# Moving a cosine product behind the value products, and dealing output products unevenly, in a fused Fourier and gated-layer kernel

## The chip, the core and the metric

The kernel runs on one core of a Trainium2 chip. The core has a matrix engine (TensorE, PE in the profile, with its weight loads as PEld), three engines for elementwise work (VectorE or DVE, ScalarE or ACT, GpSimd or POOL) and SyncE (SP), which issues most transfers. Each engine works through its own queue in order; they wait for each other by semaphores. The metric is the device time in microseconds (us), as the median of several runs.

## The reference

```python
X = np.fft.fft(x, axis=1)              # x: 8 sequences x 3008 rows x 256
X = np.fft.fft(X, axis=2)
x = X.real.reshape(24064, 256)
gate = np.maximum(x @ w_gate, 0.0)     # 256 x 1536
val = x @ w_val                        # 256 x 1536
out = gate * val @ w_out               # 1536 x 256
```

So a two-dimensional Fourier transform, of which the real part is kept, then a gated layer with a ReLU on the gate.

## The kernel before

**Folding.** The transform along the 256 channels is folded into the weights, so that gate and value are made from two arrays for each sequence, U (cosine part of the transform along the rows) and V (sine part): WA and WB are the weights combined with the cosine and sine of the channels, WM is -2 times WB. Row s and its mirror row S-s have the same cosine part and opposite sine parts. So each *tile*, 128 of the 1536 hidden columns by a block of 512 or 481 rows, yields both the rows and their mirror rows: the value of the rows is WA·U + WB·V, and with one more product, the **mirror product** (`mirror`, line 880, WM·V added to the same PSUM bank), it becomes that of the mirror rows. In PSUM a bank holds 128 x 512 numbers; `v` has two banks, `p` two, `o` two, `g` and `d` one each.

**Order of the work.** Sequence b (0 to 7) has three blocks of rows (512, 512, 481; sequence 0 has four smaller segments and another code path), and a block has 12 tiles, numbered from 0. From sequence 1 on, each tile is one call of `slot`, in which parts of four tiles are interleaved by hand: `cur`, whose value is made, `mid`, the next, `nxt`, after it, whose gate is made, and `after`, whose gate is seeded. In TensorE's queue a call puts, in this order:

- the sine product of the gate of `nxt` (`sine_part`, line 1020), which ScalarE copies out (line 1023)
- a first share of **output products** (line 782, 256 columns each): the block before, times w_out. They wait for nothing near by, and are dealt to the tiles by `outs`, of which five eighths, rounded down, go here
- the cosine product of the gate of `nxt` (`cosine_part`, line 1027), onto a seed that ScalarE wrote (`seed`, line 1015)
- where `mid` is *short* (below): its cosine product (`value_cosine`, line 1045)
- the mirror product of the tile before (`pending`, line 880)
- the value products of `cur` (lines 874 and 875)
- the rest of the output products

VectorE follows with the second half of `pending` and the first half of `cur` (both line 910: ReLU of the gate, times the value), then one step of the gate of `nxt` (`both`, line 1031), to which GpSimd adds (line 1032). The mirror product of a tile changes the bank that its first half reads, so it has to wait for that half.

**Short tiles.** In the last four blocks, three tiles each are short: their value takes two products instead of three. ScalarE seeds bank `d` (`seed_value`, line 1041), `value_cosine` adds WA·U and ScalarE keeps twice the result (line 1046); in the tile's own call `value_sine` (line 1050) adds the sine part; the mirror half is made by subtraction (line 1055, VectorE) and a product on GpSimd (line 1056). `outs` is corrected by one or two products around a short tile.

**Other work between tiles.** During the first two blocks of sequences 2 to 6 the row transform of the next sequence is made: after tiles 0, 2, 6, 8 three products each (line 586), and in tiles 3, 4, 9, 10 one *sum* each on VectorE (line 598 and the like). `run_one(evict)` copies a finished output bank to SBUF (line 795), and SP sends it out (line 807).

`per_tile` is the number of output products that wait, divided by 12 and rounded up. A 512-row block leaves 96 of them, 8 a tile; a 481-row block leaves 84 or, when enough remaining rows of several sequences have come together, 96.

Of the kernel before, what the change touches and what calls it, by code (L numbers as in the profile page):

```python
# [34 lines left out]
def kernel(  # L35
# [815 lines left out]
    def run(todo, n):  # L851
        for _ in range(min(n, len(todo))):
            todo.pop(0)()
        if not paired:
            flush()

    def run_one(todo):
        if todo:
            todo.pop(0)()
# [12 lines left out]
    def two(bank, st, i):  # L872

        nc.tensor.matmul(bank[:, 0:st["n"]], lhsT=WA[i][:, st["f"]], rhs=st["us"], start=True, stop=False)  # L874
        nc.tensor.matmul(bank[:, 0:st["n"]], lhsT=WB[i][:, st["f"]], rhs=st["vs"], start=False, stop=True)  # L875

    def mirror(bank, st, i):

        W, v = (WB, st["vm"]) if st["b"] == 0 else (WM, st["vs"])
        nc.tensor.matmul(bank[:, 0:st["n"]], lhsT=W[i][:, st["f"]], rhs=v, start=False, stop=True, skip_group_check=True)  # L880

    def bank(tag):
        return {"g": psG, "p": psP, "v": psV, "d": psD}[tag].tile([128, 512], F32, name=tag, tag=tag)

    def space():
        return rp.tile([128, 512], F32, name="r", tag="r", bufs=12)
# [26 lines left out]
    def second(st):  # L913
        (relu_mult if "s" in st else mult)(st, 1)
        if st["n"] == 481:
            keep_rest(st)
# [5 lines left out]
    def value(st):  # L922
        st["v"] = bank("v")
        two(st["v"], st, 1)

    def gate(st, tag="g"):
        st["g"] = bank(tag)
        two(st["g"], st, 0)
        relu(st)
# [80 lines left out]
    def seed(st, p=None):  # L1010

        if st is None or st["kind"] == "o":
            return
        st["p"] = p or bank("p")
        nc.scalar.activation(st["p"][:, 0:st["n"]], st["c"], ACTF.Copy, scale=b2[:, st["fi"]:st["fi"] + 1])  # L1015

    def sine_part(st):
        n = st["n"]
        st["g"] = bank("g")
        nc.tensor.matmul(st["g"][:, 0:n], lhsT=WM[0][:, st["f"]], rhs=st["vs"], start=True, stop=True)  # L1020
        q = space()
        st["s"] = q, space(), q
        nc.scalar.copy(q[:, 0:n], st["g"][:, 0:n])  # L1023

    def cosine_part(st):
        n = st["n"]
        nc.tensor.matmul(st["p"][:, 0:n], lhsT=WA[0][:, st["f"]], rhs=st["us"], start=False, stop=True, skip_group_check=True)  # L1027
# [15 lines left out]
    def value_cosine(st):  # L1043
        n, st["a"] = st["n"], space()
        nc.tensor.matmul(st["v"][:, 0:n], lhsT=WA[1][:, st["f"]], rhs=st["us"], start=False, stop=True, skip_group_check=True)  # L1045
        nc.scalar.mul(st["a"][:, 0:n], st["v"][:, 0:n], 2.0)
# [5 lines left out]
    def value_second(st):  # L1052
        n = st["n"]
        a = st["a"][:, 0:n]
        nc.vector.tensor_tensor(a, a, st["v"][:, 0:n], op=ALU.subtract)
        nc.gpsimd.tensor_tensor(half_h(st, 1), st["s"][2][:, 0:n], a, op=ALU.mult)
        if n == 481:
            keep_rest(st)

    def slot(cur, mid, nxt, after, outs, fold_us):  # L1060

        outs += cur["short"] + (pending is not None and pending.get("short", False)) - 2 * (mid is not None and mid["short"])
        stop = len(todo_out)

        def out(part):
            run(todo_out, len(todo_out) - stop + outs * part // 8)
        old = nxt is not None and nxt["kind"] == "o"
        new = nxt is not None and nxt["kind"] == "n"
        if old:
            gate(nxt)  # L1070
        lead = cur["lead"]
        out(4 if lead else 0)
        if new and mid["kind"] != "o":
            sine_part(nxt)
        out(4 if lead else 5)
        if new and mid["kind"] == "o":
            sine_part(nxt)
        if new and not lead:
            cosine_part(nxt)
        if not lead:  # L1080
            seed(after)
        if mid is not None and mid["short"]:
            value_cosine(mid)
        if pending is not None and pending.get("short"):
            value_second(pending)
        elif pending is not None:
            mirror(pending["v"], pending, 1)
            second(pending)
        if cur["short"]:
            value_sine(cur)  # L1090
        else:
            value(cur)
        if cur["kind"] == "o":
            mult(cur, 0, cur["first"])
        else:
            relu_mult(cur, 0)
        if lead:
            out(5)
            cosine_part(nxt)
            seed(after)  # L1100
        if new:
            both(nxt)
        if old:
            nxt["first"] = nxt["r"]
            mirror(nxt["g"], nxt, 0)
            relu(nxt)
        if cur["short"]:
            sm = cur["s"][2][:, 0:cur["n"]]
            nc.scalar.activation(sm, sm, ACTF.Relu)
        if nxt is not None and nxt["short"]:  # L1110
            seed_value(nxt)
        run_fold(fold_us)
        run_one(evict)
        run_one(sums)
        out(8)
        return cur
# [4 lines left out]
    for b in range(B):  # L1121
# [4 lines left out]
        for blk, block in enumerate(blocks):  # L1126
# [42 lines left out]
            per_tile = -(-len(todo_out) // NF)  # L1169
            paired = b > 0  # L1170
            if (b, blk) == (0, 0):
                for fi in range(NF):
                    st = tile_of(block, fi, (U, V, CB))
                    add_h(st, hs)
                    if fi == 8:
                        todo_out = out_steps(b, block, hs, True)
                    pending = first_tile(st, more.get((0, fi), ()), 6)
                mirror(pending["g"], pending, 0)
                relu(pending)
            elif not paired:  # L1180
                for fi in range(NF):
                    st = tile_of(block, fi, (U, V, CB))
                    add_h(st, hs)
                    tag = {(3, 8): "g", (3, 9): "d", (3, 10): "g", (3, 11): "d"}.get((blk, fi), "p")
                    last = []
                    if (blk, fi) == (3, 11):
                        last = [lambda: (sine_part(ahead[1]), cosine_part(ahead[1]), both(ahead[1]), seed(ahead[2]))]
                    if (blk, fi) == (3, 9):
                        ahead = [next(tiles) for _ in range(3)]
                        more[(3, 9)] += [lambda: seed(ahead[0], prime())]  # L1190
                        more[(3, 10)] += [lambda: seed(ahead[1], prime())]
                        more[(3, 11)] += [lambda: (sine_part(ahead[0]), cosine_part(ahead[0]), both(ahead[0]))]
                    if (blk, fi) == (1, 8):
                        run(todo_out, len(todo_out))
                        todo_out = out_steps(b, block, hs, True)
                    pending = single_tile(st, 3 if blk == 1 else per_tile // 2, more_b.get((blk, fi), ()), last, tag)
                    run(todo_dft, DFT_0[blk - 1][fi])
            else:
                for fi in range(NF):
                    at = NF * blk + fi  # L1200
                    cur = ahead.pop(0)
                    add_h(cur, hs)
                    ahead.append(next(tiles, None))
                    outs = per_tile
                    if (b, blk) == (B - 1, 2) and fi > 8:
                        outs = (10, 11, 17)[fi - 9]
                        if fi == 9:
                            rest = out_steps(b, block, hs)
                            early, rest = rest[:10] + rest[12:16], rest[10:12] + rest[16:]
                            todo_out += early  # L1210
                    if (b, at) in ((2, 5), (2, 9), (2, 13)):
                        f = slice(128 * (at - 5), 128 * (at - 1))
                        nc.scalar.mul(WV[:, f], WM[1][:, f], -0.5)
                    if (b, at) == (5, 0):
                        nc.sync.dma_start(out=WB[0][0:1, :], in_=WM[0][0:1, :])
                    if (b, at) == (6, 24):
                        open_bank()
                    pending = slot(cur, *ahead, outs, .72)
                    for step in more_1.get(at, ()) if b == 1 else ():
                        step()  # L1220
                    run(todo_dft, DFT_1[at] if b == 1 else DFT_EVEN[at])
# [44 lines left out]
```

## Time and profile before

| | us |
|---|---|
| median of three runs | 628.22 (628.15 to 628.43) |
| the profiled execution, whole | 628.35 |
| its span, first to last instruction | 626.6 |
| TensorE busy | 618.7 |
| VectorE busy | 550.3 |
| GpSimd busy | 516.4 |
| ScalarE busy | 462.8 |

The span is one execution, from the first to the last instruction; the whole time has 1.75 us around it. Busy is the time in which an engine had at least one instruction under way. TensorE's instructions overlap each other, so that its busy time can hide waits. In the timeline, a row has the start in us, the duration, the engine, the line of the kernel, the operation with what it writes and reads, the number of merged instructions (x3) and, in brackets, counted idle time before it and what ended it.

### The profile page before, as it was taken

What the parts mean: (1) busy time and instruction counts of PE and PEld (TensorE: products, weight loads), DVE (VectorE), ACT (ScalarE), POOL (GpSimd) and SP (SyncE); (2) the same over time, 40 slices, a digit from 0 to 9 for tenths busy, and PEclk for the clock granted to TensorE, in tenths of its full rate; (3) what the DMA queues carried; (4) which work ended last, traced back from release to release, by engine and by line L of the source; (5) the groups of instructions that cost most, each with busy time, mean ns of one, the idle gap of its engine ahead of it and who ended that gap; (6) DMA issues with size and microseconds to landing.
All of it is one profiled execution on the core that took longest, in us unless ns stands there. A gap on an engine that the chain in (4) does not pass through costs nothing.

```text
span 626.6 us, 12437 instructions
## 1 busy us (share of the span) xinstructions
PE 618.7 (99%) x4091; PEld 397.6 (63%) x4091; DVE 550.3 (88%) x979; ACT 462.8 (74%) x853; POOL 516.4 (82%) x490
## 2 busy tenths in 40 slices
PE   8999999999999999999999999999999999999997
PEld 2566666566666666666666666666666666666666
DVE  8886676999899999988999899899999989999991
ACT  7796667767778777776777777777777768999882
POOL 8988992898899988799979989799896656888780
PEclk9999999999999999999999999999999999999999
DMA  9955758734364427315362425211211111211113
GB/s 241 210 206 124 175 181 99 190 65 147 86 148 145 125 76 191 107 44 166 80 190 65 141 76 122 61 53 50 77 52 46 43 60 37 62 51 51 51 44 104
DMA packets 86035, 66.48 MB, mean 106 GB/s; under 512 B 41639, under 2 KB 69063, under 8 KB 85970
## 3 DMA queue, kind: packets, MB, share of 16 engines
q1 hardware_dynamic: 81384, 60.02, 35.2%
q0 software_dynamic: 3984, 4.92, 3.9%
q10 hardware_dynamic: 602, 0.75, 0.4%
q8 instruction: 32, 0.52, 0.3%
q14 instruction: 33, 0.27, 0.1%
HBM read 41.89 MB, written 34.17 MB: 121 GB/s over the span
## 4 chain that ended last, share of the span: by engine, by line
PE 92%; DVE 4%; ACT 2%; issue 1%; DMA 1%; DVEq 0%; ACTq 0%
PE o L782 36%; PE v L880 10%; PE v L875 9%; PE v L874 9%; PE g L1020 8%; PE p L1027 8%; PE d L586 4%; DVE h L910 2%; PE p L880 1%; PE p L874 1%; PE p L875 1%; DVE r L1031 1%; PE v L395 1%; PE d L1045 1%; DMA XG<-in_x_dram 1%
## 5 line engine op out<-in xcount | busy, mean ns | idle before, releaser
L1032 POOL TENSOR_TENSOR r<-r 128x512 f32<-128x512 f32 (+1 forms) x251 | 312.8, 1253 | 85.9 <-DVE r L1031 84.5
L910 DVE SCALAR_TENSOR_TENSOR h<-r,v 128x512 bf16<-128x512 f32 (+1 forms) x478 | 303.3, 674 | 38.5 <-PE v L880 26.8
L782 PE MATMUL o<-wo,h 128*128 128x256 bf16 x2172 | 330.8, 272 | 0.0
L782 PEld LDWEIGHTS <-h 128*128 128x128 bf16 x2220 | 216.8, 98 | 112.2 <-issue 1.3
L1015 ACT ACTIVATE p<-CB,b 128x512 f32<-128x512 bf16 (+1 forms) x251 | 171.9, 685 | 65.7 <-DVE r L1031 63.4
L1023 ACT COPY r<-g 128x512 f32<-128x512 f32 (+1 forms) x251 | 144.7, 577 | 55.4 <-PE g L1020 47.2
L1031 DVE SCALAR_TENSOR_TENSOR r<-r,p 128x512 f32<-128x512 f32 (+1 forms) x251 | 168.3, 670 | 0.6 <-ACT r L1023 0.6
L875 PE MATMUL v<-V,WB 128*128 128x512 bf16 (+3 forms) x284 | 104.1, 367 | 0.0
L874 PE MATMUL v<-U,WA 128*128 128x512 bf16 (+3 forms) x284 | 104.1, 367 | 0.0
L1020 PE MATMUL g<-V,WM 128*128 128x512 bf16 (+1 forms) x251 | 94.1, 375 | 0.2
L1027 PE MATMUL p<-U,WA 128*128 128x512 bf16 (+1 forms) x251 | 94.1, 375 | 0.0
L880 PE MATMUL v<-V,WM 128*128 128x512 bf16 (+1 forms) x240 | 89.9, 375 | 0.8 <-DVE h L910 0.4
L899 DVE TENSOR_TENSOR h<-r,v 128x376 bf16<-128x376 f32 (+2 forms) x90 | 46.0, 546 | 17.4 <-PE v L880 8.3
L874 PEld LDWEIGHTS <-WA 128*128 128x128 bf16 x336 | 32.7, 97 | 37.2 <-issue 10.7
L795 ACT COPY os<-o 128x512 f32<-128x512 f32 x92 | 52.5, 571 | 3.2 <-PE o L782 3.2
L198 POOL TENSOR_TENSOR XG<-XG,XD 128x510 f32<-128x510 f32 x42 | 53.0, 1271 | 0.4 <-DMA XG<-xr 0.4
L875 PEld LDWEIGHTS <-WB 128*128 128x128 bf16 x336 | 32.8, 97 | 32.3 <-ACT WB L678 0.2
L890 ACT ACTIVATE r<-p 128x376 f32<-128x376 f32 (+1 forms) x80 | 38.0, 486 | 17.8 <-PE p L880 9.6
L206 POOL TENSOR_TENSOR AA<-XG 128x510 f32<-128x510 f32 x42 | 45.4, 1090 | 0.0
L1020 PEld LDWEIGHTS <-WM 128*128 128x128 bf16 x251 | 24.6, 98 | 5.7 <-issue 0.3
L880 PEld LDWEIGHTS <-WM 128*128 128x128 bf16 x241 | 23.6, 98 | 5.5 <-issue 2.4
L1027 PEld LDWEIGHTS <-WA 128*128 128x128 bf16 x251 | 24.6, 98 | 3.3 <-issue 0.2
(196 smaller groups left out, 479.1 us busy)
## 6 DMA issues: line engine op xcount, KB each, us to landing
out_dram<-os SPq DMA_DIRECT2D x124, 128.0 KB
xr<-in_x_dram SPq DMA_DIRECT2D x12, 768.0 KB
XG<-xr SPq DMA_DIRECT2D x12, 768.0 KB
XD<-in_x_dram SPq DMA_DIRECT2D x15, 512.0 KB
out_dram<-os SPq DMA_DIRECT2D x35, 112.0 KB
XD<-in_x_dram SPq DMA_DIRECT2D x8, 448.0 KB
CB<-ch SPq DMA_DIRECT2D x7, 376.2 KB
out_dram<-os SPq DMA_DIRECT2D x13, 96.0 KB
```

Of the source, the lines that this page charges most:

```text
L198: e.tensor_tensor(XG[p, r, t, ::-1, 1:D], XG[p, r, t, ::-1, 1:D], XD[p, r, t, :, D - 1:0:-1], op=ALU.add)
L782: nc.tensor.matmul(st["p"][0:m, q, :], lhsT=lhs(f), rhs=wo[:, f, :], start=(f == 0 and not (early and q)), stop=(f == NF - 1), skip_group_ ...
L874: nc.tensor.matmul(bank[:, 0:st["n"]], lhsT=WA[i][:, st["f"]], rhs=st["us"], start=True, stop=False)
L875: nc.tensor.matmul(bank[:, 0:st["n"]], lhsT=WB[i][:, st["f"]], rhs=st["vs"], start=False, stop=True)
L880: nc.tensor.matmul(bank[:, 0:st["n"]], lhsT=W[i][:, st["f"]], rhs=v, start=False, stop=True, skip_group_check=True)
L910: nc.vector.scalar_tensor_tensor(half_h(st, sign), in0=st["s"][1 + sign][:, 0:n], scalar=0.0, in1=st["v"][:, 0:n], op0=ALU.max, op1=ALU.mult)
L1015: nc.scalar.activation(st["p"][:, 0:st["n"]], st["c"], ACTF.Copy, scale=b2[:, st["fi"]:st["fi"] + 1])
L1020: nc.tensor.matmul(st["g"][:, 0:n], lhsT=WM[0][:, st["f"]], rhs=st["vs"], start=True, stop=True)
L1023: nc.scalar.copy(q[:, 0:n], st["g"][:, 0:n])
L1027: nc.tensor.matmul(st["p"][:, 0:n], lhsT=WA[0][:, st["f"]], rhs=st["us"], start=False, stop=True, skip_group_check=True)
L1031: nc.vector.scalar_tensor_tensor(sp[:, 0:n], in0=q[:, 0:n], scalar=-0.5, in1=st["p"][:, 0:n], op0=ALU.mult, op1=ALU.add)
L1032: nc.gpsimd.tensor_tensor(sm[:, 0:n], sp[:, 0:n], q[:, 0:n], op=ALU.add)
```

## The change

Three things. `value_cosine(mid)` is issued after the value products of `cur` and no longer ahead of the mirror product of `pending`. In blocks where `per_tile` is 7, the tiles get 5, 7, 5, 9, 9 and 7 output products in turn. In the last block, the last three tiles get 10, 9 and 19 in place of 10, 11 and 17 (the first of them one more, as it follows a short tile), and in the last two tiles of all, which have no `nxt`, four eighths instead of five go ahead of the mirror product.

```diff
@@ slot @@
-        out(4 if lead else 5)
+        out(4 if lead or nxt is None else 5)
...
         if not lead:
             seed(after)
-        if mid is not None and mid["short"]:
-            value_cosine(mid)
         if pending is not None and pending.get("short"):
             value_second(pending)
...
             value_sine(cur)
         else:
             value(cur)
+        if mid is not None and mid["short"]:
+            value_cosine(mid)
         if cur["kind"] == "o":
@@ the loop over tiles @@
-                    outs = per_tile
+                    outs = per_tile + ((-2, 0, -2, 2, 2, 0)[fi % 6] if per_tile == 7 else 0)
                     if (b, blk) == (B - 1, 2) and fi > 8:
-                        outs = (10, 11, 17)[fi - 9]
+                        outs = (10, 9, 19)[fi - 9]
```

## The prediction

> **What bounds the kernel now.** I read the page's busy rows first, then who waited for the mirror product (line 880), then the timeline of TensorE and of VectorE around it.
>
> ```profile
> span 626.6 us, 12437 instructions
> PE 618.7 (99%) x4091; PEld 397.6 (63%) x4091; DVE 550.3 (88%) x979; ACT 462.8 (74%) x853; POOL 516.4 (82%) x490
> ```
>
> ```profile
>   DVE h L910: 0.4, 2
> ```
>
> The third line is from the answer on line 880: TensorE sat idle 0.4 us, in two places, until VectorE's line 910 was done. By these rows hardly anything can be won. The timeline says otherwise. Its columns are start, duration, engine, line. It shows tiles 3 to 6, and the last one, of the first block of sequence 4.
>
> ```profile
> 332.20 0.38 PE L880 MATMUL v<-V,WM 128*128 128x512 bf16 x1
> 332.42 0.38 PE L874 MATMUL v<-U,WA 128*128 128x512 bf16 x1
> ...
> 333.39 0.60 PE L782 MATMUL o<-wo,h 128*128 128x256 bf16 x4
> 333.83 0.38 PE L1027 MATMUL p<-U,WA 128*128 128x512 bf16 x1
> 334.04 0.38 PE L880 MATMUL v<-V,WM 128*128 128x512 bf16 x1
> ...
> 335.67 0.38 PE L1027 MATMUL p<-U,WA 128*128 128x512 bf16 x1
> 336.08 0.38 PE L880 MATMUL v<-V,WM 128*128 128x512 bf16 x1
> ...
> 337.70 0.38 PE L1027 MATMUL p<-U,WA 128*128 128x512 bf16 x1
> 338.13 0.38 PE L880 MATMUL v<-V,WM 128*128 128x512 bf16 x1
> ...
> 348.10 0.38 PE L1027 MATMUL p<-U,WA 128*128 128x512 bf16 x1
> 348.51 0.38 PE L880 MATMUL v<-V,WM 128*128 128x512 bf16 x1
> ...
> 350.24 0.38 PE L1027 MATMUL p<-U,WA 128*128 128x512 bf16 x1
> 350.56 0.38 PE L880 MATMUL v<-V,WM 128*128 128x512 bf16 x1
> ```
>
> Products of 512 columns start 0.216 us apart (332.20 to 332.42) though each lasts 0.38, and four output products take 0.44, so 0.109 each. What counts is thus the spacing of starts. From 333.83 to the mirror at 334.04 is 0.21: no wait. But 335.67 to 336.08 is 0.41, a wait of 0.194; the next mirror waits 0.214, and those at 348.51 and 350.56 wait 0.194 and 0.104: **0.71 us in this block**, nearly all of it under the tail of the product before, where no idle is counted. The cause is on VectorE:
>
> ```profile
> 328.52 1.28 DVE L910 SCALAR_TENSOR_TENSOR h<-r,v 128x512 bf16<-128x512 f32 x2 [0.47 <-PE v L880]
> ...
> 332.69 1.28 DVE L910 SCALAR_TENSOR_TENSOR h<-r,v 128x512 bf16<-128x512 f32 x2 [0.45 <-PE v L880]
> 333.89 0.68 DVE L1031 SCALAR_TENSOR_TENSOR r<-r,p 128x512 f32<-128x512 f32 x1
> 334.49 0.34 DVE L598 SCALAR_TENSOR_TENSOR V<-es,d 128x188 bf16<-128x188 f32 x1
> 334.75 1.28 DVE L910 SCALAR_TENSOR_TENSOR h<-r,v 128x512 bf16<-128x512 f32 x2
> ...
> 336.80 1.28 DVE L910 SCALAR_TENSOR_TENSOR h<-r,v 128x512 bf16<-128x512 f32 x2
> ```
>
> Each pair on line 910 is the second half of the tile before and the first half of the tile's own; the next mirror adds into the bank that the first half reads, so it can't start before. A plain round is: mirror to pair 0.49 (332.20 to 332.69), pair 1.28, pair to mirror 0.05 (336.03 to 336.08), together **1.82**. TensorE needs 1.84 for a tile with seven output products (332.20 to 334.04): just enough. In tiles 3 and 4 a sum of the transform (line 598) follows line 1031, VectorE runs without a gap from 332.69 to 338.08, and the mirrors of tiles 5 and 6 come 3.88 and 5.93 after 332.20, where TensorE by itself would take 3.69 and 5.53.
>
> By the Trainium skill, "Perfetto Trace Analysis", section Identifying the Most-Contended Engine, matmul busy time is a bad measure of how near a kernel is to its limit, since matmuls are pipelined. The trace agrees here: 99% busy, and yet 0.71 us lost in one block.
>
> **Blocks with seven products a tile.** Twelve tiles at 7 become 5, 7, 5, 9, 9, 7, twice; the sum stays 84, and nothing is added on any engine. Five eighths, rounded down, go ahead of the mirror (3, 4, 3, 5, 5, 4), the rest behind it (2, 3, 2, 4, 4, 3). From one mirror to the next TensorE then has, counted from the mirror of tile 3: to tile 4 nine products, 1.84+0.22=2.06; to tile 5 eight, 1.95; to tile 6 six, 1.73. So it reaches mirror 5 after 4.01, later than the 3.88 of VectorE: no wait. It reaches mirror 6 after 5.74 where VectorE gives 5.93: 0.19. VectorE's chain isn't put off by this: the pair at 334.75 is 2.55 after 332.20, and the later mirror 4 allows it at 2.06+0.49=2.55, with nothing to spare. From tile 9 to the next block's first: 2.06+1.95+1.95 (3 and 5 of the next block) =5.96 against the same 5.93: no wait. The price is in the thinned tiles: from tile 1 to 2 and from 7 to 8 only six products stand, 1.73 against the round of 1.82, 0.09 each. (In the row at 328.52 the pair ends at 329.80, so today such a mirror could start at 329.85; with seven it comes 0.02 later.) The tiles behind which transform products run have 0.48 more and don't wait. At the first tile, where pieces of 481 and 512 columns mix, one product less costs 0 to 0.11; I take 0.05. After: 0.19+0.09+0.09+0.05=0.42. **Gain 0.29 a block.** Only blocks whose 84 output products come from a 481-column piece without a rest have seven a tile: sequences 2, 4 and 6. Taken alike, 0.86.
>
> Against this change speaks the Trainium skill, "TensorE: Matmul & The Clock Gate", section Back-to-back issue gap: it gives some 131 ns between matmuls of 512 columns in a sustained stream with weight loads. By that a tile of six would, as an estimate, be 0.42 shorter and its mirror would wait 0.5, not 0.09. The trace doesn't agree: 0.216 (332.20 to 332.42). So it gets no chance.
>
> **Cosine product behind the value.** Twelve tiles are short. In the tile before each, line 1045 leaves the place between cosine (1027) and mirror (880) for that behind line 875. No instruction is added. First, one of the middle, and last:
>
> ```profile
> 524.37 0.37 PE L1027 MATMUL p<-U,WA 128*128 128x481 bf16 x1
> 524.62 0.36 PE L1045 MATMUL d<-U,WA 128*128 128x481 bf16 x1
> ...
> 554.28 0.38 PE L1027 MATMUL p<-U,WA 128*128 128x512 bf16 x1
> 554.62 0.38 PE L1045 MATMUL d<-U,WA 128*128 128x512 bf16 x1
> 554.84 0.38 PE L880 MATMUL v<-V,WM 128*128 128x512 bf16 x1
> ...
> 604.00 0.37 PE L1027 MATMUL p<-U,WA 128*128 128x481 bf16 x1
> 604.43 0.36 PE L1045 MATMUL d<-U,WA 128*128 128x481 bf16 x1
> ```
>
> ```profile
> 553.90 0.67 ACT L1041 ACTIVATE d<-CB,b 128x512 f32<-128x512 bf16 x1
> ...
> 555.80 0.58 ACT L1046 ACTIVATE r<-d 128x512 f32<-128x512 f32 x1
> ```
>
> ```profile
> 523.37 1.26 DVE L910 SCALAR_TENSOR_TENSOR h<-r,v 128x512 bf16<-128x512 f32 x2
> ...
> 553.25 1.28 DVE L910 SCALAR_TENSOR_TENSOR h<-r,v 128x512 bf16<-128x512 f32 x2
> ...
> 603.58 0.65 DVE L910 SCALAR_TENSOR_TENSOR h<-r,v 128x481 bf16<-128x481 f32 x1
> ```
>
> Line 1045 waits 0.05, 0.12 and 0.23 today (start less the cosine's start less 0.203 or 0.216), for ScalarE's seed on line 1041 (553.90+0.67=554.57, and 0.05). In its new place, three products later, it waits for nothing. But it was also the mirror's cover. The mirror will now wait for the pair of line 910: 524.63+0.05, 554.53+0.05, 604.23+0.05, against its free start of 524.57, 554.50, 604.20: 0.11, 0.09, 0.08. The same over all twelve: the three tiles of sequence 6 go from 0.10 to 0.27, the six of sequence 7's first two blocks from 0.66 to 0.51, the last three from 0.56 to 0.27. Together 1.33 to 1.05; **gain 0.27**. Behind the waiting mirror stand the value products, line 1045 and output products; the pair of VectorE that waits for it comes earlier than now, since 0.216 of TensorE's work has left its front. The doubling on line 1046 would be the next to be late: line 1045 starts at 554.58+0.65=555.23, ends 555.61, and ScalarE comes to line 1046 at 555.80: covered by 0.14. Bounds, as no row shows a mirror uncovered there: all 1.33 gained if it never waited, 12 times 0.21 = 2.5 lost if it started no earlier than today.
>
> **The last tiles.** Their remaining 39 products are dealt 11, 9, 19 instead of 11, 11, 17, and the last two tiles put 4 and 9 of theirs ahead of the mirror instead of 6 and 10.
>
> ```profile
> 608.84 1.36 PE L782 MATMUL o<-wo,h 128*128 128x256 bf16 x11
> 610.04 0.37 PE L880 MATMUL v<-V,WM 128*128 128x481 bf16 x1
> ...
> 612.28 0.37 PE L880 MATMUL v<-V,WM 128*128 128x481 bf16 x1
> ...
> 614.04 0.36 PE L880 MATMUL v<-V,WM 128*128 128x481 bf16 x1 [0.21 <-DVE h L910]
> ```
>
> ```profile
> 609.27 0.65 DVE L910 SCALAR_TENSOR_TENSOR h<-r,v 128x481 bf16<-128x481 f32 x1
> ...
> 612.76 1.23 DVE L910 SCALAR_TENSOR_TENSOR h<-r,v 128x481 bf16<-128x481 f32 x2 [1.02 <-PE v L880]
> ```
>
> With 9 for 11 the first mirror is free at 609.82 and waits for VectorE until 609.92+0.05=609.97. Three products of 0.203 and 14 of 0.109 later the second comes at 612.11; with 10 products behind it (7 now) TensorE is at 613.81 for the last, VectorE allows 612.11+0.48+1.23+0.05=613.87. That is 0.17 ahead of 614.04, and the same products follow. **Gain 0.17**; SP's output transfers move by as little.
>
> **Sum.** 0.86+0.27+0.17=1.30. The profiled execution took 628.35 (span 626.6 and 1.75 around it), so 627.05; it lies 0.13 above the median of 628.22, so **626.9**. 0.2%, about what a measurement of this kernel can tell from no change, is 1.26: the forecast lies on that border.
>
> **Rivals.**
> - Waits only change places (0.15): if the second half of a block kept the 0.19 that the first keeps, or the thinned tiles lost their whole 0.11, the blocks give 0.1 each or nothing, and the time is 627.5 to 627.8. For it: no margin at 2.55. Against: 5.96 over 5.93.
> - The mirror without cover (0.06): if line 910 in the tile before ends later than it does now, the mirror's new wait exceeds the old one. From 0.023 on the twelve tiles lose on balance (1.05 against 1.33, over 12), from 0.11 on the whole change; at the bound of 2.5 lost the time is 628.2+2.5-0.86-0.17=629.7, slower. For it: sequence 6 loses already. Against: the pair follows a mirror in each round.
> - Full recovery (0.05): neither thinned tiles nor mirrors wait, only the 0.19 in mid-block stays: 3 times 0.52, 1.33 and 0.38 won, 625.0. Against: the round of 1.82.
> - Only counted idle comes back (0.04): the 0.4 of the second fence, at most 627.8. Against: the starts.
> - The forecast (0.70): 626.5 to 627.3 by itself.
>
> The range takes in forecast and the first rival: 626.3 to 627.9. Faster by over 0.2%: 0.45 of the forecast and full recovery, 0.50; within: the other 0.25 of it, the first and fourth rivals, 0.44; slower: 0.06.
>
> **What will show it.** In the first blocks of sequences 2, 4, 6 mirrors 5, 11 and the next block's first follow their cosine by 0.21, mirror 6 by 0.41, mirrors 2 and 8 by 0.31. Line 1045 follows line 875 by 0.21, and mirrors of those tiles wait 0.06 to 0.12. The last mirror starts 0.17 sooner against its block. It would be wrong if VectorE's pairs move, or the sine or cosine products begin to wait for ScalarE.

## The result, and the profile after

| | before | after |
|---|---|---|
| median of 16 runs each, us | 628.25 | 627.07 |
| lowest to highest | 627.98 to 628.73 | 626.81 to 627.31 |
| the profiled execution, us | 628.35 | 626.96 |
| its span | 626.6 | 625.2 |

The ratio after to before is 0.998, with a 95% interval of 0.9973 to 0.9987. So the changed kernel is faster, by 1.18 us or 0.19%, where 1.30 us was forecast. By the two timelines all three parts work, and each is worth about what was forecast for its stage.

TensorE in the timeline of the changed kernel, the same stretch of the first block of sequence 4 (tiles 1 to 6, then the first mirror of the next block; start, duration, engine, line). Mirror 3 is here the mirror product that the call of tile 3 issues, and so on:

```profile
329.04 0.38 PE L1027 MATMUL p<-U,WA 128*128 128x512 bf16 x1
329.34 0.38 PE L880 MATMUL v<-V,WM 128*128 128x512 bf16 x1
...
331.67 0.38 PE L880 MATMUL v<-V,WM 128*128 128x512 bf16 x1
...
332.31 0.60 PE L782 MATMUL o<-wo,h 128*128 128x256 bf16 x4
332.97 0.71 PE L782 MATMUL o<-wo,h 128*128 128x256 bf16 x5
333.51 0.38 PE L1027 MATMUL p<-U,WA 128*128 128x512 bf16 x1
333.73 0.38 PE L880 MATMUL v<-V,WM 128*128 128x512 bf16 x1
...
335.46 0.38 PE L1027 MATMUL p<-U,WA 128*128 128x512 bf16 x1
335.68 0.38 PE L880 MATMUL v<-V,WM 128*128 128x512 bf16 x1
...
337.20 0.38 PE L1027 MATMUL p<-U,WA 128*128 128x512 bf16 x1
337.61 0.38 PE L880 MATMUL v<-V,WM 128*128 128x512 bf16 x1
...
349.72 0.38 PE L1027 MATMUL p<-U,WA 128*128 128x512 bf16 x1
349.94 0.38 PE L880 MATMUL v<-V,WM 128*128 128x512 bf16 x1
```

Four and five output products now stand between the mirrors of tiles 3 and 4, 2.06 us apart (331.67 to 333.73). Mirror 5 follows its cosine product by 0.22 and doesn't wait; mirror 6 still comes 0.41 behind its cosine, a wait of 0.19; the next block's first (349.94) doesn't wait. The price stands at 329.34: the thinned tile's mirror comes 0.30 behind its cosine, a wait of 0.09. VectorE in the same stretch:

```profile
332.15 1.29 DVE L910 SCALAR_TENSOR_TENSOR h<-r,v 128x512 bf16<-128x512 f32 x2 [0.45 <-PE v L880]
...
334.22 1.28 DVE L910 SCALAR_TENSOR_TENSOR h<-r,v 128x512 bf16<-128x512 f32 x2
...
336.28 1.28 DVE L910 SCALAR_TENSOR_TENSOR h<-r,v 128x512 bf16<-128x512 f32 x2
```

From mirror 3 (331.67) to the end of the third pair (337.56) and 0.05 more is 5.94, as before. VectorE does the same work in the same time; TensorE has done two output products more by then (23 for 21). The calls just ahead of a short tile's own, first, one of the middle, and last:

```profile
523.45 0.37 PE L1027 MATMUL p<-U,WA 128*128 128x481 bf16 x1
523.76 0.36 PE L880 MATMUL v<-V,WM 128*128 128x481 bf16 x1
...
553.54 0.38 PE L1027 MATMUL p<-U,WA 128*128 128x512 bf16 x1
553.85 0.38 PE L880 MATMUL v<-V,WM 128*128 128x512 bf16 x1
554.28 0.38 PE L875 MATMUL v<-V,WB 128*128 128x512 bf16 x1
554.50 0.38 PE L1045 MATMUL d<-U,WA 128*128 128x512 bf16 x1
...
602.96 0.37 PE L1027 MATMUL p<-U,WA 128*128 128x481 bf16 x1
603.24 0.36 PE L880 MATMUL v<-V,WM 128*128 128x481 bf16 x1
```

Line 1045 follows line 875 by 0.22, without a wait. The mirrors wait 0.11, 0.09 and 0.08 (start less the cosine's start, less 0.203 for 481 columns or 0.216 for 512). And the end:

```profile
607.64 1.15 PE L782 MATMUL o<-wo,h 128*128 128x256 bf16 x9
608.77 0.36 PE L880 MATMUL v<-V,WM 128*128 128x481 bf16 x1
609.38 1.69 PE L782 MATMUL o<-wo,h 128*128 128x256 bf16 x14
610.91 0.37 PE L880 MATMUL v<-V,WM 128*128 128x481 bf16 x1
611.52 1.25 PE L782 MATMUL o<-wo,h 128*128 128x256 bf16 x10
612.66 0.36 PE L880 MATMUL v<-V,WM 128*128 128x481 bf16 x1
```

By the spacing of 0.109, nine products from 607.64 leave TensorE free at 608.62; the mirror starts at 608.77, a wait of 0.15. Ten from 611.52 leave it free at 612.61, and the last mirror waits 0.05.

How far the changed kernel is ahead of the one before at the same mirror of both traces shows where the time came from:

| up to | ahead, us | gained in the stage | forecast |
|---|---|---|---|
| before sequence 2 | 0.06 | 0.06 | 0 |
| end of the first block of sequence 2 | 0.34 | 0.28 | 0.29 |
| the same of sequence 4 | 0.62 | 0.28 | 0.29 |
| the same of sequence 6 | 0.91 | 0.28 | 0.29 |
| the last short tile | 1.20 | 0.28 | 0.27 |
| the last mirror | 1.38 | 0.18 | 0.17 |

Between these stages the lead stays the same within 0.01. The 0.06 ahead of the first stage is a difference of the two executions, not of the kernels, whose programs are the same up to there. (The changed kernel's page counts 4046 matmuls beside 4091 weight loads: 45 records are missing, so its busy sum isn't set beside the other's.)

### The profile page after: what moved, and what is told of

Read it like the earlier page. It is cut to its first block, busy times and chain, and to the rows that moved or that the text cites. A ratio compares the mean times of both kernels' runs of the same rounds, so it can differ in the third digit from the quotient of the medians.

```text
span 625.2 us, 12392 instructions
## 1 busy us (share of the span) xinstructions
PE 615.5 (98%) x4046; PEld 396.9 (63%) x4091; DVE 548.9 (88%) x979; ACT 463.7 (74%) x853; POOL 515.9 (83%) x490
## 4 chain that ended last, share of the span: by engine, by line
PE 95%; DVE 1%; issue 1%; POOL 1%; DMA 1%; ACT 1%; DVEq 0%; POOLq 0%; ACTq 0%
PE o L782 38%; PE v L875 10%; PE v L880 10%; PE g L1020 9%; PE p L1027 8%; PE v L874 8%; PE d L586 4%; PE p L880 1%; PE p L874 1%; DMA XG<-in_x_dram,gidx 1%; PE p L875 1%; DVE h L899 1%; PE o L427 1%; POOL XG L120 1%; PE g L586 0%
## 5 line engine op out<-in xcount | busy, mean ns | idle before, releaser
L874 PE MATMUL v<-U,WA 128*128 128x512 bf16 (+3 forms) x245 | 89.3, 365 | 0.0
```

## The experiments

The theory: VectorE's round from mirror to mirror, and its dense chain beside a sum, set when a mirror may start, and an output product put between two mirrors fills 0.109 of a wait and no more. The rivals: the gain came from one part alone; waits only change places; the new order on TensorE, not VectorE, makes the mirrors wait.

**The value's cosine product alone.** The kernel before, with this part only:

```diff
-        if mid is not None and mid["short"]:
-            value_cosine(mid)
...
             value(cur)
+        if mid is not None and mid["short"]:
+            value_cosine(mid)
```

> The value's cosine product moved behind line 875, nothing else of the change. Theory (VectorE's round of 1.82 us sets the mirror): line 1045 no longer waits (1.33 us in twelve tiles before), the mirror of the same tiles waits 0.06 to 0.12 instead, 1.05 in all: 0.27 us faster than the kernel before, a loss of 0.17 in sequence 6 against a gain of 0.44 in sequence 7. Rival (the move is what brings the whole gain, the output products nothing): 1.2 us faster. Rival (mirror without cover): slower.

Measured: 628.11 against 628.53 of the kernel before in the same batch, ratio 0.9992 (0.9983 to 1.0001); by the times alone that can't be told from no change, though a gain of 1.2 us (0.9981) lies outside the interval. The timeline, of the same middle tile:

```profile
554.62 0.38 PE L1027 MATMUL p<-U,WA 128*128 128x512 bf16 x1
554.92 0.38 PE L880 MATMUL v<-V,WM 128*128 128x512 bf16 x1
555.57 0.38 PE L1045 MATMUL d<-U,WA 128*128 128x512 bf16 x1
```

The mirror waits 0.09, line 1045 not at all, and over the twelve tiles 1.03 us of waits of mirrors stand where 1.33 of line 1045 stood. That is the theory's price for this part. The move neither brings the whole gain nor a loss.

**The blocks alone.**

```diff
-                    outs = per_tile
+                    outs = per_tile + ((-2, 0, -2, 2, 2, 0)[fi % 6] if per_tile == 7 else 0)
```

> Only the uneven dealing in the three blocks with seven products a tile. Theory: per block the waits of four mirrors (0.19, 0.21, 0.19, 0.10) become one of 0.19 and three of 0.05, 0.09, 0.09: 0.28 us a block, 0.85 us faster than the kernel before. Rival (waits only change places): under 0.3 us faster, with the four old mirrors still waiting or the thinned tiles waiting 0.2 and more.

Measured: 627.73 against 628.53, ratio 0.9987 (0.9978 to 0.9996). In sequence 4 the mirrors wait 0.06, 0.09, 0.19 and 0.09, 0.43 in all against 0.70, and 0.42 in sequence 6. The waits shrink and don't merely change places.

**The end alone.**

```diff
-        out(4 if lead else 5)
+        out(4 if lead or nxt is None else 5)
...
-                        outs = (10, 11, 17)[fi - 9]
+                        outs = (10, 9, 19)[fi - 9]
```

> Only the new dealing and shares in the last three tiles. Theory: the mirror of tile 9 waits 0.15, the last 0.05 instead of 0.38: 0.18 us faster than the kernel before. Rival (the end is set by the last transfers): no difference in the last mirror's time to the end of the span is expected, but the span wouldn't shrink.

Measured: 628.27 against 628.53, ratio 0.9995 (0.9986 to 1.0004), which leaves it open by the times. The timeline has the two waits as expected: TensorE is free of the nine products at 610.25, of the ten at 614.24.

```profile
609.27 1.15 PE L782 MATMUL o<-wo,h 128*128 128x256 bf16 x9
610.40 0.36 PE L880 MATMUL v<-V,WM 128*128 128x481 bf16 x1
...
613.15 1.25 PE L782 MATMUL o<-wo,h 128*128 128x256 bf16 x10
614.29 0.36 PE L880 MATMUL v<-V,WM 128*128 128x481 bf16 x1
```

The rival is settled by the traces: from the last mirror's start to the end of the span it is 12.55 us in the kernel before, 12.56 here and 12.54 in the changed kernel, so the end moves with the mirror. (The span of this execution, 626.9, is longer than the 626.6 before, but it was 0.5 behind at the mirror of 116 us already, where the programs are the same; from there to the last mirror it gained 0.26.)

**One product more in front of the uncovered mirror.** The changed kernel, with:

```diff
-        out(4 if lead or nxt is None else 5)
+        out(4 if lead or nxt is None else 6 if mid["short"] else 5)
```

> The changed kernel, with six eighths instead of five of a tile's output products ahead of the mirror where the next tile is short (4 and 2 instead of 3 and 3). Theory: the round between the two mirrors gets one product of 0.109 more and 1.73 becomes 1.84, so the twelve waits of 0.06 to 0.12 vanish but for some 0.03 in all: 1.0 us faster than the changed kernel, 626.0. Rival (the uncovered mirror waits because of the new order on TensorE, not for VectorE's pair): the waits stay, 627.1.

Measured: 626.22, ratio to the kernel before 0.9964 (0.995 to 0.9977); the changed kernel's ratio is 0.998, so it is 0.0016 or 1.0 us ahead of that one. All twelve waits are gone from the trace; two of 0.05 have come up in the last block ahead of the sine product (line 1020), 0.11 in all where the expectation had 0.03. The same middle tile:

```profile
552.84 0.60 PE L782 MATMUL o<-wo,h 128*128 128x256 bf16 x4
553.28 0.38 PE L1027 MATMUL p<-U,WA 128*128 128x512 bf16 x1
553.50 0.38 PE L880 MATMUL v<-V,WM 128*128 128x512 bf16 x1
554.14 0.38 PE L1045 MATMUL d<-U,WA 128*128 128x512 bf16 x1
```

Cosine, mirror, value products and line 1045 stand in the order of the changed kernel, so that order didn't make the mirror wait: one product of 0.109 was missing in the round.

**The dealing turned round.** The changed kernel, with:

```diff
-                    outs = per_tile + ((-2, 0, -2, 2, 2, 0)[fi % 6] if per_tile == 7 else 0)
+                    outs = per_tile + ((2, 0, 2, -2, -2, 0)[fi % 6] if per_tile == 7 else 0)
```

> The changed kernel with the dealing of the seven-product blocks turned round: 9, 7, 9, 5, 5, 7, so that tiles with transform products get more and tiles with sums fewer. Same products, same sum of 84. Theory: VectorE's dense chain still puts mirrors 4, 5 and 6 at 1.82, 3.88 and 5.93 behind mirror 3, and with fewer products in between they wait 0.20, 0.32, 0.10, and the same in the block's second half: 1.24 us a block instead of 0.42, 2.5 us slower than the changed kernel, 629.5. Rival (it doesn't matter where the products stand, the gain came from elsewhere): 627.1.

Measured: 629.57, ratio to the kernel before 1.0019 (1.001 to 1.0028): slower than the kernel before, and by the ratios 2.5 us slower than the changed kernel. Mirrors 4, 5 and 6 of the same block:

```profile
334.51 0.38 PE L1027 MATMUL p<-U,WA 128*128 128x512 bf16 x1
334.93 0.38 PE L880 MATMUL v<-V,WM 128*128 128x512 bf16 x1
336.44 0.38 PE L1027 MATMUL p<-U,WA 128*128 128x512 bf16 x1
336.99 0.38 PE L880 MATMUL v<-V,WM 128*128 128x512 bf16 x1 [0.16 <-DVE h L910]
338.72 0.38 PE L1027 MATMUL p<-U,WA 128*128 128x512 bf16 x1
339.04 0.38 PE L880 MATMUL v<-V,WM 128*128 128x512 bf16 x1
```

They wait 0.20, 0.33 and 0.10. Only in the longest is part of it counted as idle, 0.16 of 0.33. So it is the place beside the sums that counts, not that the dealing is uneven.

**More ahead of the mirror, without the move.** The kernel before, with:

```diff
-        out(4 if lead else 5)
+        out(4 if lead else 6 if mid is not None and mid["short"] else 5)
```

> The kernel before, value's cosine product in its old place, with six eighths ahead where the next tile is short. Theory: line 1045 comes one product of 0.109 later and its waits for ScalarE's seed fall from 1.33 to 0.3 in all, without a wait of the mirror: 1.0 us faster than the kernel before; so the waits could be filled without the move. Rival (line 1045 waits for something that comes later when it is later): no gain.

Measured: 627.59 against 628.51, ratio 0.9986 (0.9977 to 0.9995), 0.92 faster. The waits of line 1045 fall from 1.33 to 0.28, with 0.11 and 0.12 left in the last two short tiles. But three new waits, 0.25 in all, stand ahead of the sine product (line 1020), so the timeline gives 0.80. So the one product alone, in the old order, wins most of what the move and the product win together: with both, as in the run with six eighths on the changed kernel, 0.11 are left of the 1.33, and here 0.53. The middle tile, and the seed that line 1045 waits for:

```profile
554.45 0.38 PE L1027 MATMUL p<-U,WA 128*128 128x512 bf16 x1
554.68 0.38 PE L1045 MATMUL d<-U,WA 128*128 128x512 bf16 x1
```

```profile
553.96 0.67 ACT L1041 ACTIVATE d<-CB,b 128x512 f32<-128x512 bf16 x1
```

The seed ends at 554.63, line 1045 starts 0.05 later: it waits for ScalarE alone. The seed starts 0.38 ahead of the cosine product in the kernel before (553.90 and 554.28) and 0.49 here: the product put in between moves TensorE by 0.11, and not the seed. One of the three new waits:

```profile
558.91 0.59 ACT L1023 COPY r<-g 128x512 f32<-128x512 f32 x1
```

```profile
559.02 0.60 PE L782 MATMUL o<-wo,h 128*128 128x256 bf16 x4
559.55 0.38 PE L1020 MATMUL g<-V,WM 128*128 128x512 bf16 x1
```

The four output products leave TensorE free at 559.46, but `g` has one bank, and ScalarE's copy of the sine product before (line 1023) ends at 559.50. In the kernel before that copy ended at 559.44 and the sine product started at 559.50, with 0.01 to spare. Here TensorE comes earlier by the wait that it has lost, ScalarE doesn't, and at three places a new wait of 0.05 to 0.10 takes up part of the gain.

**Shares written out for the seven-product blocks.** The kernel with six eighths, and `slot` taking the number ahead of the mirror:

```diff
-            run(todo_out, len(todo_out) - stop + outs * part // 8)
+            run(todo_out, len(todo_out) - stop + (first if first and 0 < part < 8 else outs * part // 8))
...
-                    outs = per_tile + ((-2, 0, -2, 2, 2, 0)[fi % 6] if per_tile == 7 else 0)
+                    outs, first = per_tile, None
+                    if per_tile == 7:
+                        first = (5, 4, 4, 4, 4, 5)[fi % 6]
+                        outs = first + (1, 3, 1, 4, 4, 3)[fi % 6]
```

> The kernel with six eighths, and in the seven-product blocks shares written out: ahead of the mirror 5, 4, 4, 4, 4, 5, behind it 1, 3, 1, 4, 4, 3. Between mirrors that leaves 8, 9, 8 products after tiles 3, 4, 5, seven between tiles 1 and 2, and five where transform products stand. Theory: none of the four waits of a block is left (0.42 a block): 1.26 us faster than the six-eighths kernel, 624.9. Rival (TensorE's sine or cosine products begin to wait for ScalarE, or output banks come free too late): waits of lines 1020, 1027 or 782 appear.

Measured: 625.01, ratio to the kernel before 0.9942 (0.9927 to 0.9958), by the ratios 1.4 us ahead of the kernel with six eighths. No mirror of the three blocks waits, and neither do lines 1020, 1027 and 782 there, so the rival falls.

**And for the eight-product blocks.**

```diff
+                    if per_tile == 8 and 0 < b < B - 1 and blk < 2:
+                        first = 5
+                        outs = first + (2, 3, 3, 4, 3, 3)[fi % 6]
```

> As the kernel with written-out shares, and in the eight-product blocks beside a transform one product moved from behind tiles 0 to behind tiles 3 (5 ahead; behind 2, 3, 3, 4, 3, 3). Theory: the waits of 0.07 and 0.10 that these blocks still have at mirror 6 and at the next block's first (about 1.1 us in all) vanish: 623.8. Rival: VectorE is so near its limit there that the waits come back elsewhere in the block: 624.9.

Measured: 623.65, ratio to the kernel before 0.9923 (0.9909 to 0.9936): faster than both kernels, by 4.9 us than the one before and, by the ratios, 3.6 us than the changed one. The waits that this was to remove add up to 1.38 in the trace of the kernel with written-out shares, more than the 1.1 expected; all of them are gone, and none has come back elsewhere. The head of its page, and mirrors 5 and 6 of the same block, 0.21 behind their cosine products, without a wait:

```profile
span 621.9 us, 12437 instructions
```

```profile
334.29 0.38 PE L1027 MATMUL p<-U,WA 128*128 128x512 bf16 x1
334.50 0.38 PE L880 MATMUL v<-V,WM 128*128 128x512 bf16 x1
336.24 0.38 PE L1027 MATMUL p<-U,WA 128*128 128x512 bf16 x1
336.45 0.38 PE L880 MATMUL v<-V,WM 128*128 128x512 bf16 x1
```

## Why the prediction was right, point by point

- **What bounds the kernel.** Waits under the tail of the product before, seen only in the spacing of starts. Right: every kernel became faster, or slower, by about the sum of such waits that it lost or gained, though the idle time counted for line 910 ahead of the mirrors was 0.4 us in all. The rival by which only counted idle comes back falls: the last kernel gained 4.9. In the table, waits are those over 0.015 us ahead of lines 880, 1045 and 1020, by the spacing of starts, from 106 us on; the kernel before has 6.54 us of them, and the gain in time is between medians of the same batch.

| kernel | waits, us | fewer by | faster by, us |
|---|---|---|---|
| changed | 5.21 | 1.33 | 1.18 |
| value's cosine product alone | 6.15 | 0.39 | 0.42 |
| blocks alone | 5.60 | 0.94 | 0.80 |
| end alone | 6.28 | 0.26 | 0.26 |
| six eighths on the changed kernel | 4.25 | 2.29 | 2.31 |
| dealing turned round | 7.76 | -1.22 | -1.06 |
| six eighths on the kernel before | 5.72 | 0.82 | 0.92 |
| shares written out, seven products | 3.02 | 3.52 | 3.50 |
| and eight products | 1.64 | 4.90 | 4.86 |

- **The blocks.** 0.29 a block was forecast, 0.28 came in each. The four waits that were to be left, 0.05, 0.09, 0.19 and 0.09, are there to 0.01, so the rival by which waits only change places falls too. The place that had nothing to spare held: VectorE's chain ran dense and wasn't put off. The 0.05 for the first tile was only a guess between 0 and 0.11; that it came out at 0.05 to 0.06 is luck.
- **The value's cosine product.** Twelve waits of 1.05 were forecast, 1.05 came, loss in sequence 6 and gain in sequence 7 included. The mirror without cover, the rival on the slower side, fell, since VectorE's pair came no later than before but for 0.01: in the middle tile 0.25 after the cosine product started in the kernel before (554.53 and 554.28), 0.26 in the changed one (553.80 and 553.54).
- **The end.** 0.17 forecast, 0.18 by the trace, 0.15 and 0.05 as the two waits.
- **Full recovery** fell with the round of 1.82, which the thinned tiles showed. The turned-round dealing showed the same round from the other side.
- **The sum.** 1.30 forecast, 1.39 between the two profiled executions, 1.18 between the medians. The terms of the trace give 1.29; the rest is the scatter of single runs, 0.5 to 0.75 us wide. The border of 1.26 that the forecast lay on was just not reached by the medians, so the side came true to which the prediction gave 0.44, not that of 0.50.
- **The spacing of products.** By the Trainium skill, "TensorE: Matmul & The Clock Gate", section Back-to-back issue gap, a sustained stream would space matmuls of 512 columns by some 131 ns. The trace of the changed kernel disagrees too (554.28 to 554.50, 0.22). The thinned tiles wait 0.09, not the 0.5 that the prediction estimated from that figure.

## What to carry to other kernels

Where an engine is busy 99% of the time, look at the spacing of its starts against the work in each instruction: a wait shorter than the pipeline's tail isn't counted as idle. Then take each round between two engines, add its links (here 0.49, 1.28 and 0.05), and set filler work between the two ends until it just covers the round. Here one product of 0.109 too few cost the 0.09 that were missing from the round. One more costs nothing in this place, but look at what the engine reaches sooner for it: with six eighths the sine product came to wait for ScalarE's copy, 0.25 in all on the kernel before and 0.11 on the changed one. Filler belongs beside the steps in which the other engine has extra work, and can be taken from steps in which this engine has extra work of its own.

## What the runs showed of the hardware that was not expected

How steady the links between engines are. In the kernel before, from VectorE's end to the start of a mirror that waited for it lie 0.053 or 0.054 us in each of the 35 waits over 0.05 from 106 us on, and from the end of ScalarE's seed to line 1045 0.050 to 0.052 in all twelve. So the three rounds beside the sums, 5.93 from mirror 3 to mirror 6 in the kernel before, took 5.94 in the changed one.
